# Softmax sums in attention: a tile moved to VectorE, a TensorE sum kept for odd units only, copies moved to ScalarE

## The chip, the cores and the metric

The kernel runs on one core of a Trainium2 chip. The metric is the time of one execution on the device in microseconds (us); with several runs, their median.

## The reference

Two rounds of the same pair of layers, in float32: attention over 2048 tokens with 32 heads of 32 columns, then a small feed-forward part for 8 chosen tokens. The change touches the attention alone.

```python
q, k, v = ...(layernorm(x) @ wqkv)            # 32 heads of 32, S = 2048, D = 1024
scores = einsum("bhqd,bhkd->bhqk", q, k) * 32 ** -0.5
p = softmax(scores, axis=-1)
x = x + einsum("bhqk,bhkd->bhqd", p, v) @ wo
x = x + (8 rows picked by a router: SwiGLU of those rows, the others get layernorm(x))
```

## The kernel before

**Units and steps.** The attention of a layer is 32 units of 16 steps. A unit `u` is a group of 4 heads and a chunk of 512 queries (`g, qc = divmod(u, 4)`); a step `s` takes one tile of 128 keys: `s = 16 * u + kt`. In step `s` TensorE makes the scores of 4 heads (`scores`, tile `pre`, L775), ScalarE turns them into `P[s]` by two exponentials of 128x1024 (L1256), and one step later TensorE multiplies `P[s]` with the values (`pv_step`, tile `pv`, L1154). In the same step TensorE also makes scores of the unit after the next (`pre_pair`, tile `st`, L736): two products, then two more, of which ScalarE takes one (`first`, L739) and VectorE three (L741, L743), for the row maxima that the exponentials of that later unit subtract. The banks of `st` are three, so a product waits until an earlier one was read; the second of the second pair waits for ScalarE's L739 of the same step.

**The sums.** Softmax also needs the sum of `P` over the keys, which are 16 tiles times 128 partitions. Tables of numbers say what is done at which step of a unit (16 and more is in the next unit). `SUMS` serves all but the last two units of a layer. A "merge" adds one tile to another by an accumulating DMA that GpSimd issues (L1192), an "add" adds a tile to the accumulator `ACC[u]` on GpSimd (128x2048, L1164). Each unit has 6 merges and 8 adds. Tile 14, with tile 15 merged in, isn't added: at step 22 (`SUM_AT`) TensorE sums it by products with ones (`sum_mm`, L1201), VectorE copies the result (`store_sum`, L1211, tile `sm`) and SyncE stores it (`sd`). Of units 0 to 28 the accumulator goes through VectorE in steps 24 to 31: four times a transposition in blocks of 32x32 (L1170, tile `turned`) and a reduction of it into `FOLD` (L1178). Once for every four units (`total`), and once after unit 28, TensorE sums `FOLD` over partitions with one product (L1186), which goes to `sd2`. At the end `sd + sd2` is inverted.

**Outputs.** One step after a unit's last tile the output `PV[u]` is copied from PSUM to tile `o` (`store_o`, L1206) and stored. This copy and that of the sum are VectorE's for units 2 to 29; for units 0, 1, 30 and 31 they are ScalarE's (`PLAIN <= u <= NU - 3`).

**Order and buffers.** The order on each engine is that in which the code issues: within a step `emit(s, "pre")`, the scores and exponentials, `pv_step`, `emit(s, "mid")`, `emit(s, "end")`. Each engine works through its queue in that order and waits at an instruction whose inputs or buffer aren't ready. `P` has 9 buffers (`PB`). A new tile gets the buffer that the program let go of first, and its exponential waits until the last reader or writer of the old tile is done, which for a tile that was merged is the landing of the DMA.

## Time and profile before

| what | us |
|---|---|
| median of 3 runs | 4354.69 |
| the runs | 4342.66, 4354.69, 4354.86 |
| the profiled execution, its own time | 4348.58 |
| its span from the first to the last instruction | 4346.8 |
| TensorE busy in the span | 4307.6 |
| VectorE, ScalarE, GpSimd busy in the span | 3045.8, 2880.2, 3270.6 |

The two attention stages lie at about 565 to 1917 us and 2719 to 4076 us of the span. TensorE's granted clock is 0.997 of full speed over the span. A busy time is the union of the instructions' records; the records of neighbours on one engine can overlap by some tens of nanoseconds, since an engine starts the next instruction before the record of the last ends. On VectorE, ScalarE and TensorE the distance from start to start is therefore the better price.

### The profile page before, as it was taken

Reading aid. Unit: us, or ns where it says so; the run is one execution under the profiler, and the core shown is the slowest. Engines: PE = TensorE matmul, PEld = TensorE weight load, DVE = VectorE, ACT = ScalarE, POOL = GpSimd, SP = SyncE. Lnnn points to the kernel's source line nnn. Section 1 sums busy time; section 2 is a strip of 40 time slices with the busy share of each in tenths; the row PEclk is TensorE's granted clock in tenths of the full one; section 3 lists DMA queues with packets and bytes.
Section 4 is the critical chain, followed back from the end, with each engine's and each line's share of the span. In section 5 each row is a group of like instructions: output and inputs, shape, how many; then the busy total and the mean of one; then the engine's idle time right before and its main releaser. Section 6 shows DMA issues by size and latency. Waiting matters only on the chain.

```text
span 4346.8 us, 75763 instructions
## 1 busy us (share of the span) xinstructions
PE 4307.6 (99%) x28255; PEld 2612.5 (60%) x28255; DVE 3045.8 (70%) x5607; ACT 2880.2 (66%) x3447; POOL 3270.6 (75%) x1367
## 2 busy tenths in 40 slices
PE   9999999999999999999999999999999999999998
PEld 7888755555555555558877787555555555555583
DVE  3322678888888898887422215888888888888863
ACT  3333289999999999960222222999999998999510
POOL 5544479999999999925634443899999999999152
PEclk9999999999999999999999999999999999999999
DMA  7877588998999989868698774999989999998698
GB/s 222 268 241 230 158 183 190 200 204 193 210 199 192 214 191 199 174 181 244 180 313 305 263 215 129 206 196 196 210 190 201 200 195 201 198 195 175 185 266 342
DMA packets 362638, 918.70 MB, mean 211 GB/s; under 512 B 48220, under 2 KB 184924, under 8 KB 305934
## 3 DMA queue, kind: packets, MB, share of 16 engines
q0 software_dynamic: 53312, 384.39, 44.2%
q1 hardware_dynamic: 291646, 490.07, 37.2%
q10 hardware_dynamic: 17312, 39.40, 3.3%
q8 instruction: 222, 3.64, 0.3%
q14 instruction: 146, 1.20, 0.1%
HBM read 395.35 MB, written 134.67 MB: 122 GB/s over the span
## 4 chain that ended last, share of the span: by engine, by line
PE 93%; DMA 3%; DVE 1%; issue 1%; POOL 1%; ACT 0%; SPq 0%; POOLq 0%; ACTq 0%; DVEq 0%
PE pv L1154 23%; PE pre L775 22%; PE st L932 17%; PE st L736 15%; PE pre L1438 6%; PE pre L932 5%; PE st L1201 1%; PE pv L567 1%; DMA wraw<-in_A_wqkv_dram 1%; PE pre L757 1%; PE pv L932 1%; DMA ord<-rd 0%; PE third L775 0%; DMA P<-P 0%; PE st L607 0%
## 5 line engine op out<-in xcount | busy, mean ns | idle before, releaser
L1164 POOL TENSOR_TENSOR acc<-acc,P 128x2048 f32<-128x2048 f32 x420 | 2058.7, 4902 | 9.4
L1256 ACT ACTIVATE P<-pre 128x1024 f32<-128x1024 f32 x2016 | 1955.1, 1024 | 24.8 <-PE pre L775 17.6
L743 DVE TENSOR_REDUCE nm<-st 128x1 f32<-128x512 f32 x1920 | 1321.0, 688 | 51.3 <-PE st L736 7.9
L775 PE MATMUL pre<-q,ks 64*128 64x512 f32 (+1 forms) x8064 | 1123.1, 395 | 2.4 <-ACT P L1256 2.4
L1154 PE MATMUL pv<-P,v 128*32 128x512 f32 x8192 | 1087.2, 605 | 0.0
L736 PE MATMUL st<-ks,q 64*128 64x512 f32 x2880 | 874.3, 432 | 2.0 <-issue 2.0
L775 PEld LDWEIGHTS pre<-q,ks 64*128 64x128 f32 (+1 forms) x8064 | 770.5, 186 | 159.9 <-ACT P L1256 32.1
L741 DVE CUSTOM_DVE_ANT_0 first<-st,first 128x512 f32<-128x512 f32 x960 | 664.0, 692 | 241.3 <-PE st L736 231.9
L739 ACT ACTIVATE first<-st 128x512 f32<-128x512 f32 x960 | 574.5, 598 | 184.4 <-PE st L736 99.6
L736 PEld LDWEIGHTS st<-dt,q 64*128 64x128 f32 x960 | 175.7, 183 | 798.2 <-DVE nm L741 727.4
L736 PEld LDWEIGHTS st<-ks,q 64*128 64x128 f32 x2880 | 487.9, 185 | 46.0 <-issue 2.3
L736 PE MATMUL st<-dt,q 64*128 64x512 f32 x960 | 476.3, 496 | 0.0
L1192 POOL DMA_DIRECT2D P<-P x366 | 373.9, 1022 | 111.3 <-PE st L736 39.6
L947 DVE TENSOR_TENSOR lo<-st,hi 128x512 fp32r<-128x512 f32 x128 | 88.4, 691 | 513.9 <-ACT hi L946 469.0
L832 POOL TENSOR_TENSOR ohl<-wraw,ord 128x2048 fp32r<-128x2048 f32 (+1 forms) x54 | 222.3, 4120 | 241.5 <-ACT ord L827 205.7
L946 ACT CAST hi<-st 128x512 fp32r<-128x512 f32 x128 | 75.2, 587 | 444.5 <-PE st L932 352.5
L832 POOL TENSOR_TENSOR wl<-wraw,wh 128x2048 fp32r<-128x2048 f32 (+1 forms) x54 | 222.5, 4123 | 170.6 <-ACT wh L831 165.2
L1154 PEld LDWEIGHTS pv<-P,v 128*32 128x32 f32 x8192 | 164.0, 108 | 263.7 <-issue 257.0
L1164 POOL TENSOR_TENSOR acc<-P 128x2048 f32<-128x2048 f32 x62 | 317.9, 5128 | 0.1
L181 POOL TENSOR_TENSOR rs<-mv,eps_c 128x1 f32<-128x1 f32 x64 | 27.7, 433 | 296.3 <-DVE mv L179 296.3
L1438 PE MATMUL pre<-woh,ohl 128*128 128x512 f32 x960 | 223.9, 390 | 3.0 <-DVE pre L1472 2.2
L1369 ACT CAST ohl<-ord 128x1024 fp32r<-128x1024 f32 x32 | 33.6, 1051 | 273.4 <-DVE ord L1360 114.3
(422 smaller groups left out, 5317.4 us busy)
## 6 DMA issues: line engine op xcount, KB each, us to landing
P<-P POOLq DMA_DIRECT2D x366, 1024.0 KB, 10.1
wraw<-in_A_wqkv_dram SPq DMA_DIRECT2D x96, 1024.0 KB
q<-qh SPq DMA_DIRECT2D x256, 128.0 KB
ks<-kh SPq DMA_DIRECT2D x112, 256.0 KB
fw<-in_B_w_down_dram SPq DMA_DIRECT2D x17, 1024.0 KB
vd<-vn SPq DMA_DIRECT2D x32, 512.0 KB
qh<-hi SPq DMA_DIRECT2D x64, 256.0 KB
ql<-lo SPq DMA_DIRECT2D x64, 256.0 KB
```

The costliest lines, as they stand in the source:

```text
L736: pe.matmul(p, Q[u][rows, i, 0, qt * 128:(qt + 1) * 128], keys, start=True, stop=True, tile_position=(64 * b, 0))
L739: act.activation(side, ps[jj], AF.Relu)
L741: dve.tensor_tensor_reduce(side, ps[jj], side, 1.0, -3.0e38, OP.add, OP.max, NM[u][:, 0, h, qt:qt + 1])
L743: dve.tensor_reduce(NM[u][:, 1 + k, h, qt:qt + 1], ps[1 - jj], axis=AX.X, op=OP.max)
L775: pe.matmul(p[:, b * 512:(b + 1) * 512], KS[(u // QC) % 2][rows, i, slot, kt * 128:(kt + 1) * 128], Q[u][rows, i, slot, :], start=(slot == ...
L832: pool.tensor_tensor(wl[:, sl], raw[:, sl], wh[:, sl].bitcast(F32), op=OP.subtract)
L932: pe.matmul(p, *pair(a, l, r), start=(a == 0 and k == 0), stop=(a == KD - 1 and k == 2))
L1154: pe.matmul(PV[u][32 * h:32 * h + 32, :], V[g, kt // 4][:, kt % 4, 32 * h:32 * h + 32], P[s][:, h, :], start=(kt == 0), stop=(kt == NT - 1 ...
L1164: (dve if on_dve else pool).tensor_tensor(o, a, P[u * NT + k].rearrange("p h c -> p (h c)"), op=OP.add)
L1192: pool.dma_start(P[u * NT + a], P[u * NT + b], accum_op=OP.add)
L1256: act.activation(P[s][:, 2 * i:2 * i + 2, :].rearrange("p h c -> p (h c)"), p, AF.Exp, scale=SCALE)
L1438: pe.matmul(p[:, bl], l[:, a, :], r[a][:, bl], start=(k == 0 and a == 0), stop=(k == 2 and a == KD - 1))
```

## The change

`SPLIT_SUMS` takes the place of `SUMS` for units 0 to 28. Tile 15 isn't merged any more: VectorE turns and reduces it straight from `P` in steps 16 to 23 (`turn` with `raw`, from `RAW_AT`), into a second `FOLD`, and `total` makes two products in one PSUM tile instead of one. The merges become 12<-11 and 14<-13 where they were 13<-12 and 14<-15. The last entry of the table, the add of tile 14, is for even units alone, which have no `sum_mm` and no stored sum any more (their places in `sd` are filled with zeros ahead of the attention). Odd units leave out that add and keep `sum_mm` of tile 14. `store_o` and `store_sum` copy on ScalarE in all units, both through tile `o`. The two lines at the end of the stage that load half of the sums move by two steps.

```diff
+SPLIT_SUMS = (
+    (3, "merge", 2, 1), (5, "merge", 4, 3), (6, "add", 0, 5), (7, "add", 6), (9, "merge", 7, 8), (9.5, "add", 2), (11, "merge", 9, 10),
+    (11.5, "add", 4), (13, "merge", 12, 11), (14, "add", 7), (15, "merge", 14, 13), (16, "add", 9), (18, "add", 12), (20, "add", 14))
+TURNED_TILE = 15
+RAW_AT = 16
...
+    sums = BEHIND_SUMS if left == 1 else SUMS if u >= TURNED else SPLIT_SUMS[:-1] if u % 2 else SPLIT_SUMS
...
+    if u >= TURNED or u % 2:
+        ev += [(SUM_AT, "mid", 5, "sum", ())]
+    if u < TURNED:
+        ev += [(at + k, "pre", 1, "turn", (k, raw)) for at, raw in ((RAW_AT, True), (TURN_AT, False)) for k in range(8)]
+        ev += [(TURN_AT + 7, "mid", 5, "total", ())]
...
-                    dve.transpose(TURN[u], ACC[u][:, 512 * h:512 * h + 512])
+                    dve.transpose(TURN[u], P[u * NT + TURNED_TILE][:, h, :] if raw else ACC[u][:, 512 * h:512 * h + 512])
...
-                pe.matmul(p, lanes, FOLD.pop(u // QC), start=True, stop=True, tile_position=(0, 0))
+                for raw in (True, False):
+                    pe.matmul(p, lanes, FOLD.pop((u // QC, raw)), start=raw, stop=not raw, tile_position=(0, 0))
...
-                (dve.tensor_copy if PLAIN <= u <= NU - 3 else act.copy)(o, PV.pop(u))
+                act.copy(o, PV.pop(u))
...
-                (dve.tensor_copy if PLAIN <= u <= NU - 3 else act.copy)(t, p)
+                act.copy(t, p)
...
-                store_sum(u, sum_mm(u), aw.tile([128, 512], F32, name="sm", bufs=1))
+                store_sum(u, sum_mm(u), aw.tile([128, 512], F32, name="o", bufs=1))
...
+            for i in range(2):
+                dma(half_of(sd, i).rearrange("(p two) c -> p (c two)", two=4), DT[i][32:64].bitcast(F32).rearrange("p a c -> p (a c)"))
...
-                if s == NS - 20:
-                    shared["first"] = aw.tile([128, 512], F32, name="sm", bufs=1)
+                if s == NS - 22:
+                    shared["first"] = aw.tile([128, 512], F32, name="o", bufs=1)
```

GpSimd, from the add of tile 4 of unit 12 (an even one) to the second merge of unit 13. Before, the tiles of unit 12 are P_10738 (4), P_10988 (11), P_11023 (12), P_11056 (13), P_10847 (7), P_11089 (14), P_11122 (15) and P_10921 (9):

```order
L1164 TENSOR_TENSOR acc_10836<-acc_10836,P_10738 128x2048
L1164 TENSOR_TENSOR acc_10836<-acc_10836,P_10988 128x2048
L1192 DMA P_11056<-P_11023 128x2048
L1164 TENSOR_TENSOR acc_10836<-acc_10836,P_10847 128x2048
L1192 DMA P_11089<-P_11122 128x2048
L1164 TENSOR_TENSOR acc_10836<-acc_10836,P_10921 128x2048
L1192 DMA P_11225<-P_11193 128x2048
L1164 TENSOR_TENSOR acc_10836<-acc_10836,P_11056 128x2048
L1192 DMA P_11289<-P_11256 128x2048
```

The same stretch of the changed kernel; here unit 12 has P_10813 (4), P_11067 (11), P_11102 (12), P_10926 (7), P_11134 (13), P_11168 (14) and P_11000 (9):

```order
L1174 TENSOR_TENSOR acc_10914<-acc_10914,P_10813 128x2048
L1204 DMA P_11102<-P_11067 128x2048
L1174 TENSOR_TENSOR acc_10914<-acc_10914,P_10926 128x2048
L1204 DMA P_11168<-P_11134 128x2048
L1174 TENSOR_TENSOR acc_10914<-acc_10914,P_11000 128x2048
L1174 TENSOR_TENSOR acc_10914<-acc_10914,P_11102 128x2048
L1204 DMA P_11310<-P_11276 128x2048
L1174 TENSOR_TENSOR acc_10914<-acc_10914,P_11168 128x2048
L1204 DMA P_11377<-P_11343 128x2048
```

The unit's last two merges have moved ahead by one add each; two adds, not one, now stand between the last of them and the next unit's first merge. In an odd unit the add of tile 14 is missing.

ScalarE, steps 6 to 8 of unit 14 (the unit after an odd one), with the semaphores waited for (DMASW is the landing of a merge, Pool is GpSimd). Before, P_11899, P_11944 and P_11985 are the steps 6, 7 and 8:

```order
L1256 ACTIVATE P_11899<-pre_11900 128x1024 [waits DMASW3_49,PE_49,Activation_49]
L1256 ACTIVATE P_11899<-pre_11906 128x1024 [waits PE_49]
L739 ACTIVATE first_11936<-st_11938 128x512 [waits PE_49]
L1256 ACTIVATE P_11944<-pre_11945 128x1024 [waits PE_49,Pool_49]
L1256 ACTIVATE P_11944<-pre_11951 128x1024 [waits PE_49]
L739 ACTIVATE first_11976<-st_11978 128x512 [waits DVE_49,PE_49]
L1256 ACTIVATE P_11985<-pre_11986 128x1024 [waits DMASW4_49,PE_49,Activation_49]
```

The same steps of the changed kernel, where they are P_11991, P_12037 and P_12078:

```order
L1270 ACTIVATE P_11991<-pre_11992 128x1024 [waits PE_49,Pool_49]
L1270 ACTIVATE P_11991<-pre_11998 128x1024 [waits PE_49]
L1223 COPY o_12019<-st_12014 128x512 [waits DMAHW1_49,PE_49,Activation_49]
L749 ACTIVATE first_12028<-st_12030 128x512 [waits PE_49]
L1270 ACTIVATE P_12037<-pre_12038 128x1024 [waits DMASW4_49,PE_49,Activation_49]
L1270 ACTIVATE P_12037<-pre_12044 128x1024 [waits PE_49]
L749 ACTIVATE first_12069<-st_12071 128x512 [waits DVE_49,PE_49]
L1270 ACTIVATE P_12078<-pre_12079 128x1024 [waits PE_49]
```

The copy of the sum stands between two steps. The landing of the unit's own first merge (2<-1, the semaphore DMASW4 in both) was waited for at step 8 and is now at step 7; after an even unit it is still at step 8.

VectorE, the first two steps after unit 13. Before (the copy of `o` stands at the end of step 0 of unit 14):

```order
L743 TENSOR_REDUCE nm<-st 128x1 x2
L741 ISA first,nm<-st,first 128x512
L741 ISA nm 128x1
L743 TENSOR_REDUCE nm<-st 128x1
L1206 COPY o<-pv 128x512
L743 TENSOR_REDUCE nm<-st 128x1
L741 ISA first,nm<-st,first 128x512
```

In the changed kernel:

```order
L753 TENSOR_REDUCE nm<-st 128x1 x2
L1181 STREAM_TRANSPOSE turned<-P 128x512
L751 ISA first,nm<-st,first 128x512
L751 ISA nm 128x1
L753 TENSOR_REDUCE nm<-st 128x1 x2
L1189 TENSOR_REDUCE fold_11274<-turned 128x4x4
L751 ISA first,nm<-st,first 128x512
```

Every step has one transposition or one reduction of it between its third maximum and the next step's first line 751, as before only the second half of a unit's steps had.

## Rows read from the trace of the kernel before

**Rows 1.** The page's busy times, and a table of windows of the steady part of the first attention stage (busy us of each engine, granted TensorE clock, share of the DMA engines, GB/s).

```profile
PE 4307.6 (99%) x28255; PEld 2612.5 (60%) x28255; DVE 3045.8 (70%) x5607; ACT 2880.2 (66%) x3447; POOL 3270.6 (75%) x1367
...
1100.00:1400.00 300.00, 300.00 (x2310) 154.29 (x2308) 265.34 (x538) 277.31 (x338) 294.76 (x99) 1.00 0.93 200
```

**Rows 2.** The chain of work that ended last, in order of time, around a `sum_mm` whose copy is VectorE's (start, us, what), and two of the steps after it.

```profile
1003.60 1.00 PE pv L1154 x8
1004.59 0.86 PE st L1201 x8
...
1007.06 1.00 PE pv L1154 x8
...
1009.66 0.99 PE pv L1154 x8
...
1012.26 1.00 PE pv L1154 x8
```

**Rows 3.** The same view at a `total`.

```profile
1113.20 1.00 PE pv L1154 x8
1114.19 0.41 PE st L1186 x2
1114.61 0.59 PE st L736 x2
...
1116.37 1.00 PE pv L1154 x8
```

**Rows 4.** The same view where ScalarE makes the copies: the output of unit 0 (first four rows), that of unit 1 (next three), the sum of unit 0 (last two).

```profile
602.38 0.99 PE pv L1154 x8
...
604.75 0.53 PE st L736 x2
605.28 0.99 PE pv L1154 x8
...
608.04 1.00 PE pv L1154 x8
...
645.46 0.99 PE pv L1154 x8
...
648.34 1.00 PE pv L1154 x8
...
650.94 1.00 PE pv L1154 x8
...
618.47 1.00 PE pv L1154 x8
...
621.95 1.06 PE pv L1154 x8
```

**Rows 5.** ScalarE's timeline at the copy of unit 0's output and at that of its sum (start, us, engine, line, instruction, and in brackets the idle time before it).

```profile
601.80 1.94 ACT L1256 ACTIVATE P<-pre 128x1024 f32<-128x1024 f32 x2
603.63 0.59 ACT L1206 COPY o<-pv 128x512 f32<-128x512 f32 x1
604.09 0.63 ACT L739 ACTIVATE first<-st 128x512 f32<-128x512 f32 x1
...
620.39 0.59 ACT L1211 COPY sm<-st 128x512 f32<-128x512 f32 x1 [0.60 <-PE st L1201]
```

**Rows 6.** A table of windows (columns as in Rows 1): steps in which VectorE turns the accumulator, then steps in which it doesn't; and VectorE's timeline over a step of the first kind.

```profile
1009.20:1030.00 20.80, 20.80 (x162) 10.62 (x161) 20.34 (x41) 19.49 (x25) 20.72 (x8) 1.00 0.62 125
1030.00:1046.00 16.00, 16.00 (x126) 8.32 (x122) 12.59 (x26) 15.23 (x20) 16.00 (x8) 1.00 1.00 220
...
1014.37 0.70 DVE L1170 STREAM_TRANSPOSE turned<-acc 128x512 f32<-128x512 f32 x1
1015.00 0.69 DVE L741 CUSTOM_DVE_ANT_0 first<-st,first 128x512 f32<-128x512 f32 x1
...
1015.62 1.44 DVE L743 TENSOR_REDUCE nm<-st 128x1 f32<-128x512 f32 x2
1016.98 0.68 DVE L1178 TENSOR_REDUCE fold<-turned 128x16 f32<-128x512 f32 x1
1017.61 0.69 DVE L741 CUSTOM_DVE_ANT_0 first<-st,first 128x512 f32<-128x512 f32 x1
```

**Rows 7.** GpSimd's timeline from a unit's add of tile 7 to the next unit's merge 2<-1.

```profile
1029.85 4.89 POOL L1164 TENSOR_TENSOR acc<-acc,P 128x2048 f32<-128x2048 f32 x1
1034.40 1.18 POOL L1192 DMA_DIRECT2D P<-P  x1
1035.02 5.17 POOL L1164 TENSOR_TENSOR acc<-acc,P 128x2048 f32<-128x2048 f32 x1
1039.94 1.08 POOL L1192 DMA_DIRECT2D P<-P  x1
```

**Rows 8.** Merges from issue to landing (the last number, us): the one issued at 1039.94, the one at 1013.65, then all of them; and who waited for a merge (us, times).

```profile
P<-P POOLq DMA_DIRECT2D x1, 1024.0 KB, 11.0
...
P<-P POOLq DMA_DIRECT2D x1, 1024.0 KB, 8.1
...
DMA to landing us min/median/max: 6.9/10.1/14.6
...
  ACT P L1256: 2.3, 4
```

**Rows 9.** ScalarE's timeline at step 7 of the unit whose merge 2<-1 is the one issued at 1039.94.

```profile
1049.05 1.94 ACT L1256 ACTIVATE P<-pre 128x1024 f32<-128x1024 f32 x2
```

More of the change, by code (lines that the diff above doesn't have):

```diff
@@ L56, with unit_events @@
     ((1, 18), (1, 21), (2, 18), (3, 3)), ((2, 14), (2, 17), (2, 20), (3, 3)))]
-def unit_events(left):
+def unit_events(u):
+    left = NU - 1 - u
     if left == 0:
@@ L63, in unit_events @@
     ev = []
-    for at, what, k, *other in (SUMS, BEHIND_SUMS)[left == 1]:
+    sums = BEHIND_SUMS if left == 1 else SUMS if u >= TURNED else SPLIT_SUMS[:-1] if u % 2 else SPLIT_SUMS
+    for at, what, k, *other in sums:
         args = (k, *other) if what == "merge" else (k, *(other or [None]), what == "vadd")
         ev.append((int(at), "end", at % 1, "merge" if what == "merge" else "add", args))
-    ev += [(SUM_AT, "mid", 5, "sum", ())]
-    if left == NU - TURNED:
-        ev += [(TURN_AT + k, "pre", 1, "turn", (k,)) for k in range(8)] + [(TURN_AT + 7, "mid", 5, "total", ())]
+    if u >= TURNED or u % 2:
[3 more added lines that the diff above has]
+        ev += [(TURN_AT + 7, "mid", 5, "total", ())]
     return ev
-EVENTS = [unit_events(i) for i in range(NU - TURNED + 1)]
+EVENTS = [unit_events(u) for u in range(NU)]
 @with_exitstack
@@ L1164, in acc_add, with turn @@
                 (dve if on_dve else pool).tensor_tensor(o, a, P[u * NT + k].rearrange("p h c -> p (h c)"), op=OP.add)
-            def turn(u, k):
+            def turn(u, k, raw):
                 h, back = divmod(k, 2)
+                key = (u // QC, raw)
                 if not back:
                     TURN[u] = aw.tile([128, 512], F32, name="turned", bufs=1)
-                    dve.transpose(TURN[u], ACC[u][:, 512 * h:512 * h + 512])
+                    dve.transpose(TURN[u], P[u * NT + TURNED_TILE][:, h, :] if raw else ACC[u][:, 512 * h:512 * h + 512])
                     return
                 if u % QC == 0 and h == 0:
-                    FOLD[u // QC] = aw.tile([128, 256], F32, name="fold", bufs=1)
+                    FOLD[key] = aw.tile([128, 256], F32, name=f"fold{int(raw)}", bufs=1)
                     if u // QC == NG - 1:
-                        dve.memset(FOLD[u // QC], 0.0)
+                        dve.memset(FOLD[key], 0.0)
                 i, j = divmod(u % QC, 2)
-                out = FOLD[u // QC].rearrange("p (i c j t h) -> p i j h t c", i=2, c=4, j=2, t=4)[:, i, j, h]
+                out = FOLD[key].rearrange("p (i c j t h) -> p i j h t c", i=2, c=4, j=2, t=4)[:, i, j, h]
                 dve.tensor_reduce(out, TURN.pop(u).rearrange("p (t c r) -> p t c r", t=4, c=4), axis=AX.X, op=OP.add)
-                if h == 3:
+                if h == 3 and not raw:
                     ACC.pop(u)
@@ L1185, in total @@
                 p = ps_st()[0:32, 0:256]
-                pe.matmul(p, lanes, FOLD.pop(u // QC), start=True, stop=True, tile_position=(0, 0))
-                t = aw.tile([128, 512], F32, name="sm", bufs=1)[0:32, 0:256]
+                for raw in (True, False):
+                    pe.matmul(p, lanes, FOLD.pop((u // QC, raw)), start=raw, stop=not raw, tile_position=(0, 0))
+                t = aw.tile([128, 256], F32, name="sm", bufs=1)[0:32]
                 dve.transpose(t, p)
@@ L1239, in emit @@
                     if 0 <= v < NU:
-                        todo += [(kt + NT * back, pri, fn, args, v) for (k, pos, pri, fn, args) in EVENTS[min(NU - 1 - v, NU - TURNED)]
+                        todo += [(kt + NT * back, pri, fn, args, v) for (k, pos, pri, fn, args) in EVENTS[v]
                                  if k == kt + NT * back and pos == where]
@@ L1247, in layer @@
             load_ones(1)
+            for i in range(2):
+                dma(half_of(sd, i).rearrange("(p two) c -> p (two c)", two=4), DT[i][32:64].bitcast(F32).rearrange("p a c -> p (a c)"))
             for i in range(2):
@@ L1270, in rest_of_step @@
                     shared["sum"] = sum_mm(NU - 1)
-                if s == NS - 20:
-                    shared["first"] = aw.tile([128, 512], F32, name="sm", bufs=1)
+                if s == NS - 22:
+                    shared["first"] = aw.tile([128, 512], F32, name="o", bufs=1)
                     sum_load(shared["first"], 0)
-                if s == NS - 17:
+                if s == NS - 19:
                     recip(shared["first"], 0)
```

## The prediction

> **What bounds the kernel now.** I read the page's busy times first, then the windows of the attention stages, then the chain of work that ended last. In the steady part of attention TensorE is busy for 300.00 us of 300 at a granted clock of 1.00 [rows 1], and the chain runs over nothing but TensorE, one product after the other. So a step costs what TensorE's products cost: 1012.26 - 1009.66 = 2.60 us from one `pv` to the next [rows 2]. I use 2.605, since neighbouring steps read 2.60 and 2.61. The others aren't far behind: in the same 300 us GpSimd is busy for 294.76, ScalarE for 277.31 and VectorE for 265.34 [rows 1]. The change takes work from TensorE and GpSimd and gives it to VectorE and ScalarE, which both release PSUM banks that TensorE writes next. The questions are what the removed products were worth, and which of the added instructions makes TensorE wait.
>
> **The sums that go.** A step with `sum_mm` takes from one `pv` to the next 1007.06 - 1003.60 = 3.46 us, and the products themselves stand in the chain with 0.86 [rows 2]. So each one left out gives 0.86 us, all of it on the path. In units 0, 2, ..., 28 that is 15 a layer, 30 in all. In unit 0 the copy was ScalarE's already, and there the step costs 0.08 more (below); gain 30 x 0.86 + 2 x 0.08 = 26.0 us.
>
> **Two products in `total`.** Now such a step takes 1116.37 - 1113.20 = 3.17, 0.56 over a plain one: 0.41 for the product and 0.16 in the next `st`, which takes 0.59 where others take 0.43 [rows 2, 3]. I read the 0.16 as a wait for a bank; a second product of the same size covers it. So I put the second at 0.41 - 0.16 = 0.25, and at most at another 0.56. There are 8 a layer: 16 x 0.25 = 4.0 us (up to 9.0).
>
> **Outputs copied by ScalarE.** Units 0 and 1 show it before the change, with the same neighbours on TensorE and ScalarE. The copy begins when the last `pv` and the exponentials are through (603.63), and the following L739 begins at 604.09 [rows 5]. The last `st` product of that step waits for this L739: the pair takes 0.53 where others take 0.24, and the step takes 605.28 - 602.38 = 2.90, the one at unit 1 648.34 - 645.46 = 2.88 [rows 4]. The step after is 2.76 in the first case and 2.60 in the second. I take 0.28 a copy, and 0.44 with the step after as the upper bound. VectorE's copies, which go, gave TensorE no wait and so give nothing back. 28 outputs a layer move (units 2 to 29): 56 x 0.28 = 15.7 us (up to 24.6). Below, the bound is zero, if in later units something else holds TensorE at that point anyway.
>
> **Sums copied by ScalarE.** Here ScalarE stands idle for 0.60 us until the sum is there [rows 5], so most of the copy lies in time that was lost anyway. From the end of one `pv` to the end of the next it is 621.95 + 1.06 - 618.47 - 1.00 = 3.54 us against 3.46 where VectorE copies [rows 2, 4]: 0.08 for each of the 28 odd units that change (3 to 29, both layers), 2.2 us. Both copies now share the one buffer `o`; between the two lie six steps, 15.6 us, for a store that SyncE issues at once.
>
> **Tile 15 on VectorE.** Eight instructions more for each of 58 units, 464 in all, less two copies of about the same length in each of units 2 to 29 (the sum copy of an even unit goes altogether). By starts, a turn and what follows it are 0.63 us apart (1014.37 to 1015.00, 1016.98 to 1017.61) [rows 6]: 5.0 us more in a unit of some 42.5. That all lies beside TensorE if a step with a turn still fits into 2.605. Steps with one show that it does: VectorE is busy there for 20.34 us of 20.80 and TensorE keeps its pace, while without turns it is 12.59 of 16.00 [rows 6], which is where the new ones go. I cost it at nothing. The cover is thin: what follows the turn (L741) holds a bank of the next step's first products, so a turn that ends late moves TensorE by as much.
>
> **GpSimd.** Odd units lose an add, 28 of 4.9 us [rows 7]; merges stay at six a unit. GpSimd isn't what bounds the step, so this gives nothing by itself. But the order of the merges changes, and with it who waits for which landing: that is the second rival.
>
> **Sum.** -26.0 + 4.0 + 15.7 + 2.2 = -4.1 us. The profiled execution took 4348.58 us (span 4346.8), so 4344.5. It lies between the runs shown and 6.1 below their median; on the median's scale the forecast is 4354.69 - 4.1 = 4350.6, that is -0.1%, which a measurement of this kernel can't tell from no change (some 0.3%, 13 us).
>
> **Rival 1: VectorE becomes the bound.** With a turn in every step its share goes from about nine tenths to 98% [rows 1, 6]. If each of the 464 new steps lost 0.05 us, that is 23.2 us: 4373.8. For: no step with a turn has had ScalarE's output copy in it yet, and an engine that never rests can't catch up after a stall. Against: eight such steps in a row already run without loss, and VectorE loses a copy in every unit. It decides from 0.04 us a step on (464 x 0.04 = 18.6, net slower than 0.3%).
> The Trainium skill (VectorE: DVE Perf Modes, The DRAIN you can't avoid) has a rule against this part: the next VectorE operation doesn't start until the pipeline of the last has emptied. By that the four long instructions of a step would take 0.69 + 1.44 + 0.69 = 2.82 us by their records, 0.2 over TensorE's step, and the change would cost an estimated 464 x 0.2 = 93 us, 4444. The starts in rows 6, 0.62 to 0.63 apart, speak against it, and so do the steps with turns; I give that no more than a small part of this rival's chance.
>
> **Rival 2: ScalarE waits for a merge.** After an odd unit the exponential of step 7 now waits for the landing of that unit's own merge 2<-1, one step earlier than before. In the trace such a merge is issued at 1039.94 and lands 11.0 us later, at 1050.94 [rows 7, 8]; the exponential of step 7 starts at 1049.05 [rows 9]. If that stays, ScalarE and behind it TensorE stop for up to 1.9 us in 28 even units (2 to 28, both layers): +53.2 us, 4403.8. Against: the merge took 11.0 us because the one before it, issued at 1034.40, was still under way. In the new order that one comes behind the add of tile 7 with one add less ahead of it, about 4.5 us earlier, and lands before 1039.94 or close to it. A merge issued with none ahead took 8.1, so it would land at 1048.0, 1 us in time; the least is 6.9 [rows 8]. What speaks for it is the spread of landings (up to 14.6) and the DMA engines' share of 0.93. It decides from landings of about 9.8 us on.
> The Trainium skill (DMA: Bandwidth & Descriptors, Anatomy of one DMA) would rule the wait out: about 2 us and the bytes at 436 GB/s, an estimated 4.4 us for such a tile, which would leave this rival no chance and the sum as it is. The trace doesn't agree: no merge took less than 6.9.
>
> **Rival 3: the output copy is hidden.** If in later units it costs TensorE nothing, the sum is -26.0 + 4.0 + 2.2 = -19.8: 4334.9. Against it stand three of four readings near 0.28.
>
> **Rival 4: even units don't become shorter.** The 0.86 us of `sum_mm` are also a pause in which ScalarE, VectorE and GpSimd catch up. GpSimd has 41.8 us of work (98.25%) in a unit of 16 x 2.605 + 0.86 = 42.5 us; an even unit keeps that work and would take 16 x 2.605 + 0.28 = 42.0. If the pause is needed, the 26 us aren't gained while the 21.9 are paid: 4376.6. Against: the odd unit behind it has one add less.
>
> **How the numbers follow.** Forecast 0.60, rival 1 0.12, rival 2 0.12, rival 3 0.10, rival 4 0.06. Predicted: 4350.6. Range: below to rival 3, 4334; above past rivals 1 and 4 to 4385, which leaves out rival 2 and the tail of rival 1. The forecast's own bounds (output copies up to 24.6, `total` up to 9.0) reach 4364.5. Faster by over 0.3% (under 4341.6): rival 3 and a little of the forecast, 0.13. Slower (over 4367.8): rivals 2 and 4 and most of rival 1, 0.27. Within: 0.60.
>
> **What would show it.** In the chain, even units without L1201 and steps of 2.6 us at their place; at each `total` two products and about 3.4 us; a step of 2.9 us after every unit. VectorE's windows near 98% busy with TensorE at 300.00 of 300. On ScalarE no exponential at step 7 that waits for a merge: if "ACT P <- DMA P<-P" in the waits is more than some us, rival 2 is right. Steps of 2.65 us or more all through, with TensorE released by L751, would be rival 1. The forecast is wrong at its root if steps between these places change their length.

## The result and the profile after

The changed kernel takes 4390.8 us (median of 6 runs, 4384.99 to 4394.46); the kernel before, run beside it, takes 4353.86. The ratio on record is 1.0098 with an interval of 1.0083 to 1.0112, that is about 43 us slower, where 4 us less were forecast. (The two medians themselves are 36.9 us apart, the two profiled executions 42.7.) The profiled execution has a span of 4389.1 us, 42.3 more than before, and all of it lies in the two attention stages.

The costs that the prediction named are there, about as large as it said. This is the chain of work that ended last, after (start, us, what): first the start of an odd unit behind an even one, then the step with `sum_mm` behind an odd unit, then a `total`.

```profile
1041.27 1.00 PE pv L1164 x8
1044.15 1.00 PE pv L1164 x8
...
1057.18 1.00 PE pv L1164 x8
1059.79 1.00 PE pv L1164 x8
1062.39 1.00 PE pv L1164 x8
...
1273.98 0.99 PE pv L1164 x8
1274.97 0.86 PE st L1213 x8
1275.83 0.43 PE st L746 x2
...
1277.59 0.99 PE pv L1164 x8
...
1123.57 0.99 PE pv L1164 x8
1124.57 0.84 PE st L1198 x4
1125.41 0.43 PE st L746 x2
...
1127.02 0.99 PE pv L1164 x8
```

The step of the output copy takes 1044.15 - 1041.27 = 2.88. Behind an even unit the steps in which the sum stood are 2.61 and 2.60 long. The step with the sum takes 3.61 (3.46 before, [rows 2]), `total` 3.45 (3.17, [rows 3]). Over both layers the medians are 2.89, 3.60 and 3.45, and of steps without any of this 2.605, as before. So by measured sizes the four terms are -26.0 + 16 x 0.28 + 56 x 0.285 + 28 x 0.13 = -1.9 us. Some 44 us are left, and they are not in these terms. Added up over both layers, the distances from one `pv` to the next are too long by 16 us at step 1, 3 at step 5 and 23 at step 7 of the third unit of each group of four, by 7 at step 8 of the second and by 3 at step 7 of the first; the kernel before lost some 6 us at steps of its own. The page, the windows and the waits of the changed kernel show what stands behind them (a group: busy us, mean ns | idle us before it and its releasers; a wait: us in total, times, longest):

```profile
PE 4321.3 (98%) x28047; PEld 2598.3 (59%) x28047; DVE 3250.1 (74%) x5961; ACT 2910.2 (66%) x3529; POOL 3141.6 (72%) x1339
...
PE 86%; DMA 7%; issue 3%; POOL 1%; ACT 1%; DVE 1%; SPq 0%; POOLq 0%; ACTq 0%; DVEq 0%
...
L1270 ACT ACTIVATE P<-pre 128x1024 f32<-128x1024 f32 x2016 | 1957.7, 1027 | 74.4 <-DMA P<-P 40.2
L1174 POOL TENSOR_TENSOR acc<-acc,P 128x2048 f32<-128x2048 f32 x392 | 1913.0, 4880 | 79.3 <-DMA P<-P 71.5
```

```profile
1100.00:1400.00 300.00, 295.18 (x2226) 148.87 (x2220) 281.08 (x562) 273.11 (x339) 270.70 (x92) 1.00 0.92 194
...
1301.30:1343.50 42.20, 42.18 (x324) 21.48 (x321) 40.87 (x83) 39.78 (x50) 40.27 (x14) 1.00 0.95 198
```

```profile
POOL acc L1174 <- DMA P<-P: 71.5, 55, 3.6
ACT P L1270 <- DMA P<-P: 40.2, 41, 2.4
```

ScalarE's exponentials waited for merges for 2.3 us before [rows 8] and wait for 40.2 now. GpSimd's adds, which hardly waited at all, wait for 71.5. In the first window (columns as in [rows 1]) TensorE is no longer busy throughout, and VectorE has 19 us of 300 left at an unchanged clock. The second is a unit without a stall: VectorE is busy for 97% of it, and TensorE for all of it. So VectorE with a turn in every step doesn't hold TensorE.

One stall, read through. GpSimd's timeline from the last merges of unit 17 to the first of unit 18 (the second and the third unit of a group of four):

```profile
1332.95 1.19 POOL L1204 DMA_DIRECT2D P<-P  x1
1333.57 5.18 POOL L1174 TENSOR_TENSOR acc<-acc,P 128x2048 f32<-128x2048 f32 x1
1338.13 1.46 POOL L1204 DMA_DIRECT2D P<-P  x1
1338.84 5.37 POOL L1174 TENSOR_TENSOR acc<-acc,P 128x2048 f32<-128x2048 f32 x1
1343.40 1.65 POOL L1204 DMA_DIRECT2D P<-P  x1
1348.69 4.57 POOL L1174 TENSOR_TENSOR acc<-acc,P 128x2048 f32<-128x2048 f32 x1 [3.64 <-DMA P<-P]
1353.72 4.61 POOL L1174 TENSOR_TENSOR acc<-acc,P 128x2048 f32<-128x2048 f32 x1 [0.47 <-DMA P<-P]
1358.25 0.87 POOL L1204 DMA_DIRECT2D P<-P  x1
```

The three merges from issue to landing (the last number, us), and SyncE's timeline over unit 17 (`ks` are keys, 256 KB a load; `dt` their differences, 64 KB):

```profile
P<-P POOLq DMA_DIRECT2D x1, 1024.0 KB, 15.6
P<-P POOLq DMA_DIRECT2D x1, 1024.0 KB, 15.5
P<-P POOLq DMA_DIRECT2D x1, 1024.0 KB, 16.0
...
1309.31 0.32 SPq L115 DMA_DIRECT2D ks<-kh  x1
1322.00 3.62 SPq L115 DMA_DIRECT2D nmx<-nmr  x4
1328.24 1.14 SPq L115 DMA_DIRECT2D q<-nmx  x2
1329.42 1.11 SPq L115 DMA_DIRECT2D ks<-kl  x1
1330.58 2.47 SPq L115 DMA_DIRECT2D ks<-kh  x2
1333.09 0.85 SPq L115 DMA_DIRECT2D ks<-kl  x1
1333.98 0.43 SPq L115 DMA_DIRECT2D ks<-kh  x1
1334.45 1.05 SPq L115 DMA_DIRECT2D dt<-kd  x2
```

In the code a unit's key loads stand one a step, from step 6 to step 13. In the trace SyncE's queue stands still behind the transfers of the row maxima (`nmx`), and then five of the six large loads and both small ones go out within some 6 us, at steps 10 to 12, beside the merges 9<-10 and 12<-11. The first units of a group show the same burst, and so does the kernel before, where only the merge 9<-10 falls beside it.

ScalarE's timeline at steps 1 and 7 of unit 18:

```profile
1348.65 1.94 ACT L1270 ACTIVATE P<-pre 128x1024 f32<-128x1024 f32 x2 [2.20 <-DMA P<-P]
...
1366.97 1.94 ACT L1270 ACTIVATE P<-pre 128x1024 f32<-128x1024 f32 x2 [1.43 <-DMA P<-P]
```

The merge 9<-10, issued at 1332.95, lands 15.6 us later at 1348.5. For this landing GpSimd's add of tile 9 waits 3.64 us and ScalarE's step 1 waits 2.20. The merge 12<-11 lands at 1353.6, and the add of tile 12 waits 0.47. Behind these adds stands the next unit's merge 2<-1: issued at 1358.25, 14.7 us after the unit's first exponential (10.0 is usual before), it lands 8.6 us later at 1366.86, and ScalarE's step 7 waits 1.43 for it. Where the kernel before passed this point, GpSimd went from one instruction to the next without a gap [rows 7].

### The profile page after: what moved, and what is told of

Read it like the earlier page. It is cut to its first block, busy times and chain, and to the rows that moved or that the text cites. A ratio compares the mean times of both kernels' runs of the same rounds, so it can differ in the third digit from the quotient of the medians.

```text
span 4389.1 us, 75570 instructions
## 1 busy us (share of the span) xinstructions
PE 4321.3 (98%) x28047; PEld 2598.3 (59%) x28047; DVE 3250.1 (74%) x5961; ACT 2910.2 (66%) x3529; POOL 3141.6 (72%) x1339
## 4 chain that ended last, share of the span: by engine, by line
PE 86%; DMA 7%; issue 3%; POOL 1%; ACT 1%; DVE 1%; SPq 0%; POOLq 0%; ACTq 0%; DVEq 0%
PE pv L1164 21%; PE pre L785 19%; PE st L942 16%; PE st L746 13%; PE pre L1452 7%; PE pre L942 5%; DMA P<-P 5%; DMA wraw<-in_A_wqkv_dram 1%; ACT P L1270 1%; PE st L1213 1%; PE pre L767 1%; PE pv L577 1%; POOL ohl L842 1%; PE pv L942 1%; POOL acc L1174 0%
## 5 line engine op out<-in xcount | busy, mean ns | idle before, releaser
L1270 ACT ACTIVATE P<-pre 128x1024 f32<-128x1024 f32 x2016 | 1957.7, 1027 | 74.4 <-DMA P<-P 40.2
L1174 POOL TENSOR_TENSOR acc<-acc,P 128x2048 f32<-128x2048 f32 x392 | 1913.0, 4880 | 79.3 <-DMA P<-P 71.5
L746 PE MATMUL st<-ks,q 64*128 64x512 f32 x2880 | 888.2, 434 | 0.0
L785 PEld LDWEIGHTS pre<-q,ks 64*128 64x128 f32 (+1 forms) x8064 | 755.5, 186 | 219.4 <-ACT P L1270 91.3
L751 DVE CUSTOM_DVE_ANT_0 first<-st,first 128x512 f32<-128x512 f32 x960 | 663.7, 691 | 69.0 <-PE st L746 66.3
L749 ACT ACTIVATE first<-st 128x512 f32<-128x512 f32 x960 | 577.7, 602 | 131.3 <-PE st L746 67.6
L1204 POOL DMA_DIRECT2D P<-P x366 | 388.1, 1060 | 215.8 <-PE st L746 136.0
L1189 DVE TENSOR_REDUCE fold<-turned 128x16 f32<-128x512 f32 x464 | 314.8, 679 | 0.1
```

Of the source, the lines that this page charges most:

```text
L746: pe.matmul(p, Q[u][rows, i, 0, qt * 128:(qt + 1) * 128], keys, start=True, stop=True, tile_position=(64 * b, 0))
L749: act.activation(side, ps[jj], AF.Relu)
L751: dve.tensor_tensor_reduce(side, ps[jj], side, 1.0, -3.0e38, OP.add, OP.max, NM[u][:, 0, h, qt:qt + 1])
L785: pe.matmul(p[:, b * 512:(b + 1) * 512], KS[(u // QC) % 2][rows, i, slot, kt * 128:(kt + 1) * 128], Q[u][rows, i, slot, :], start=(slot == ...
L1174: (dve if on_dve else pool).tensor_tensor(o, a, P[u * NT + k].rearrange("p h c -> p (h c)"), op=OP.add)
L1204: pool.dma_start(P[u * NT + a], P[u * NT + b], accum_op=OP.add)
```

## The experiments

Two theories were put first. **M**: the merges land late and ScalarE waits for their buffers. **V**: VectorE is full. From the second set on, **G** stood beside M: GpSimd falls behind by itself, for want of a pause in even units. Times below are ratios to the kernel before on the same chip, with their interval; "us" is the ratio less 1, of 4350. The last two columns are the waits of ScalarE's exponentials and of GpSimd's adds for merges, in the profiled execution.

| run | ratio | us | ScalarE waits | GpSimd waits |
|---|---|---|---|---|
| changed kernel | 1.0098 (1.0083 to 1.0112) | +43 | 40.2 | 71.5 |
| e1_copies_back | 1.0103 (1.0084 to 1.0123) | +45 | 43.1 | 67.6 |
| e2_copies_alone | 1.0034 (1.0023 to 1.0046) | +15 | none shown | none shown |
| e3_copy_behind | 1.0080 (1.0062 to 1.0098) | +35 | 29.3 | 69.6 |
| e4_no_key_loads | 1.0017 (1.0007 to 1.0027) | +7 | 9.5 | 11.4 |
| e5_keys_early | 1.0232 (1.0213 to 1.0251) | +101 | 78.6 | none shown |
| e6_five_merges | 1.0150 (1.0129 to 1.0172) | +65 | 53.5 | 25.6 |
| e7_before_no_keys | 0.9989 (0.9979 to 0.9998) | -5 | 1.5 | none shown |
| e8_sum_in_all | 1.0077 (1.0060 to 1.0094) | +33 | 15.5 | 44.1 |
| e9_keys_spread | 1.0138 (1.0121 to 1.0155) | +60 | 48.3 | 6.8 |
| e10_merge_first | 1.0193 (1.0176 to 1.0210) | +84 | 73.0 | 7.3 |
| e11_spread_behind | 1.0082 (1.0066 to 1.0099) | +36 | 37.3 | 10.1 |
| e12_keys_late_behind | 1.0068 (1.0054 to 1.0083) | +30 | 28.5 | 40.9 |
| e13_keys_late | 1.0056 (1.0041 to 1.0072) | +24 | 22.9 | 39.1 |
| e14_keys_late_behind_sums | 1.0070 (1.0056 to 1.0084) | +30 | 26.3 | 43.2 |
| e15_keys_later | 1.0009 (1.0000 to 1.0018) | +4 | 12.8 | 22.1 |
| e16_keys_placed | 1.0114 (1.0099 to 1.0129) | +50 | 43.0 | 43.7 |
| e17_keys_off_first | 1.0105 (1.0090 to 1.0120) | +46 | 49.3 | 44.6 |

A second table shows the mechanism (first layer, medians over units 4 to 27, worked out from GpSimd's and ScalarE's timelines): how long the merges 9<-10, 12<-11 and 14<-13 of a group's second unit take to land (before: 9<-10, 13<-12, 14<-15), and when the merge 2<-1 of the third unit is issued after that unit's first exponential, and how long it takes.

| run | landings, us | merge 2<-1 issued at | lands after |
|---|---|---|---|
| before | 13.8, 8.7, 10.5 | 10.0 | 10.4 |
| changed kernel | 14.4, 14.6, 14.9 | 14.0 | 8.7 |
| e4_no_key_loads | 8.0, 7.9, 8.5 | 10.4 | 7.3 |
| e6_five_merges | 14.8, 14.9 | 14.6 | 7.1 |
| e9_keys_spread | 12.2, 11.8, 12.1 | 11.1 | 8.7 |
| e10_merge_first | 9.8, 9.8, 11.5 | 10.3 | 10.1 |
| e16_keys_placed | 14.0, 14.0, not shown | 13.0 | 9.4 |

### The copies

**e1_copies_back** gives the copies of outputs and sums back to VectorE in the changed kernel, **e2_copies_alone** moves them to ScalarE in the kernel before, **e3_copy_behind** puts the output copy of the changed kernel behind the next step's L749.

```diff
-                act.copy(o, PV.pop(u))
+                (dve.tensor_copy if PLAIN <= u <= NU - 3 else act.copy)(o, PV.pop(u))
```

```diff
+                if held:                      # e3: one step later, behind pre_pair(*pr, 0, side)
+                    store_o(held.pop(), aw.tile([128, 512], F32, name="o", bufs=1))
```

> The changed kernel with the copies of outputs and sums back on VectorE (for units 2 to 29), the rest as changed. Theory M (ScalarE waits for P buffers until merges land, some 44 us; ScalarE's copies cost 0.28 and 0.13 us a piece): 56 x 0.28 + 28 x 0.13 = 19 us come back if VectorE still has room for the copies beside a turn in every step, so about 4372 against 4391; the waits for landings stay. Rival V (VectorE is full and that is where the time went): two copies of 0.6 us more a unit lengthen it, up to 56 x 0.6 + 28 x 0.6 = 50 us slower than the changed kernel, about 4441, and the waits name VectorE.

> The kernel before with only the copies moved to ScalarE. Theory M with the copies at 0.28 and 0.13 us: 56 x (0.28 + 0.13) = 23 us slower than before, about 4377, a step of 2.9 us after every unit. Rival C (the copies cost more in later units than in units 0 and 1, and are behind most of the 44 us not forecast): 50 us or more slower, 4405. If a copy is hidden in later units: 4354.

> The changed kernel with the copy of the output issued behind the next step's L749 instead of ahead of it, so that L749 isn't late. Theory M: the 0.28 us a unit shrink to 0.1 or less, 56 x 0.2 = 11 us faster than the changed kernel, about 4380; the waits for landings stay. Rival: the copy costs the same wherever it stands in ScalarE's queue, 4391; or the next pv waits for its bank and it costs more.

e2 costs 15 us (10 to 20 by the interval; 23 were expected), with steps of 2.89 behind each unit and 3.55 at each sum: about the price that the prediction gave the copies, in a kernel without a stall. e1 gains nothing, and neither of its two forecasts came. The waits for merges stay, and where VectorE turns in every step its copy costs as much as ScalarE's. VectorE's timeline in e1 at an output copy:

```profile
1130.13 0.69 DVE L751 CUSTOM_DVE_ANT_0 first<-st,first 128x512 f32<-128x512 f32 x1
...
1131.35 0.68 DVE L1218 COPY o<-pv 128x512 f32<-128x512 f32 x1
1131.95 0.68 DVE L753 TENSOR_REDUCE nm<-st 128x1 f32<-128x512 f32 x1
1132.55 0.68 DVE L1189 TENSOR_REDUCE fold<-turned 128x16 f32<-128x512 f32 x1
1133.14 0.68 DVE L751 CUSTOM_DVE_ANT_0 first<-st,first 128x512 f32<-128x512 f32 x1
```

From one L751 to the next it is 3.01 us there instead of 2.60, and the step of TensorE behind it is about 2.95 long. So one step with a copy and a turn is too much for VectorE, while a turn in every step is not: theory V holds for that step alone. e3 comes out 8 us lower, where 11 were expected, but the intervals overlap. The copy itself got cheaper by less: the two steps at a unit's end take 2.66 and 2.76 where they took 2.89 and 2.60, which is 0.07 less, some 4 us for 56 units.

### Loads, and GpSimd's pause

**e4_no_key_loads** leaves out the loads of the keys of groups 2 to 7 in the changed kernel (the attention of these groups then works with keys of earlier ones); **e7_before_no_keys** does so in the kernel before.

```diff
-                if g + 1 < NG:
+                if g + 1 < 2:
                     if qc < 2:
                         loads.extend((load_k, g + 1, h, i) for h in (2 * qc, 2 * qc + 1) for i in range(3))
```

> The changed kernel without the loads of keys (and of their differences) for the head groups 2 to 7 of each layer: the keys of groups 0 and 1 are used again, so the attention of the later groups isn't the reference's. Those loads run in units 0 and 1 of each four. Theory M with the loads as a part of the cause (stalls are seen in units 1 and 2 of each four): merges land in time, most of the 44 us come back, 4345 to 4360. If the closer merges alone are the cause, the stalls stay where they are: 4385 to 4391. Rival V: no change, 4391.

> Control: the kernel before without the key loads of groups 2 to 7 (the attention of those groups then works with the keys of earlier ones, so its result is another). Theory M: before, the loads meet only merges four steps apart at the end of a unit and cost next to nothing, so 4338 to 4346, at most 8 us less than the kernel before; the loss of 35 us to the loads belongs to the new order of merges. Rival (the loads cost time in both kernels alike): some 30 us less than before, about 4315.

Without these loads the changed kernel loses 7 us instead of 43, its merges land after 8 us even where they stand two steps apart, and the waits nearly go:

```profile
POOL acc L1174 <- DMA P<-P: 11.4, 9, 2.4
ACT P L1270 <- DMA P<-P: 9.5, 7, 2.3
```

What is left of the waits is beside loads too: the loads of group 1, in the first two units of each layer, stay in e4, and all nine waits of GpSimd's adds and 7.1 of ScalarE's 9.5 us lie in the second and third unit of a layer. The kernel before gains only 5 us by the same. So neither the new order of the merges nor the loads are enough: it takes both. e4 also speaks against G by itself: with the same adds in even units, but without loads, the merge 2<-1 goes out 10.3 to 10.5 us after its unit's first exponential in every kind of unit. And it rules out that VectorE's new instructions lengthen the landings, since e4 has them all.

**e8_sum_in_all** uses the short table in all units (TensorE sums tile 14 everywhere, GpSimd has an add less); **e6_five_merges** fills GpSimd's pause in odd units with the add of tile 13 in place of the merge 14<-13; **e10_merge_first** turns GpSimd's order.

```diff
-    sums = BEHIND_SUMS if left == 1 else SUMS if u >= TURNED else SPLIT_SUMS[:-1] if u % 2 else SPLIT_SUMS
+    sums = BEHIND_SUMS if left == 1 else SUMS if u >= TURNED else SPLIT_SUMS[:-1]             # e8
+    sums = BEHIND_SUMS if left == 1 else SUMS if u >= TURNED else ODD_SUMS if u % 2 else SPLIT_SUMS   # e6
...
-    (11.5, "add", 4), (13, "merge", 12, 11), (14, "add", 7), (15, "merge", 14, 13), (16, "add", 9), (18, "add", 12), (20, "add", 14))
+    (11.5, "add", 4), (13, "merge", 12, 11), (14, "add", 7), (15, "add", 13), (16, "add", 9), (18, "add", 12))                # e6, ODD_SUMS
+    (11.5, "add", 4), (13, "merge", 12, 11), (14, "add", 7), (15, "merge", 14, 13), (16, "add", 9), (19.5, "add", 12), (21.5, "add", 14))   # e10
```

> The changed kernel with the short table in all units: TensorE sums tile 14 in even units too (two copies of sums on ScalarE instead of one in two units), and GpSimd has one add less in every unit. It gives back the 26 us gain of the sums and about 2 us for their copies. Theory M: the merges stand where they stood, so the landings in units 0 and 1 of each group stay at 13 to 16 us and the stalls stay, less what GpSimd makes good by being early: 4395 to 4420. Rival G: GpSimd has 5 us of pause in every unit, the stalls of some 44 us go, and the time is 4370 to 4378.

> The changed kernel with five merges instead of six in odd units: tile 13 isn't merged into 14, GpSimd adds it in the time that the add left out in odd units leaves. Theory M: a seventh of a unit's bytes less in every second unit, so the stalls after odd units (steps 1 and 7 of the unit behind) go and those inside unit 1 of a group get smaller; half to three quarters of the 44 us, 4358 to 4370. Rival G: odd units lose the pause that GpSimd had there, all units then hold 98% work for it, and the time rises, above 4395.

> The changed kernel with GpSimd's order turned at one place: the next unit's merge 2<-1 stands ahead of the add of tile 12 and its merge 4<-3 ahead of the add of tile 14 (the adds move from steps 18 and 20 to 19.5 and 21.5). Bytes, landings and loads stay. Theory M+G: the merge 2<-1 no longer waits behind an add that waits for a landing, it is issued at its usual time in all units, and the stalls at step 7 and 8 go: 4350 to 4370, less what the tiles 12 and 14, which are held some 5 us longer, cost at other steps. Rival (ScalarE waits because the landings themselves are long): 4385 or more.

e8, at 4382.6 between the two forecasts, speaks for G as much as for M. It pays back the 26 us of the sums and 4 for their copies and by its ratio is still 9 us faster than the changed kernel (the intervals overlap; but it has 30 us more work on TensorE and isn't slower). In the second unit its merge 9<-10 takes 14.1 us (14.4 in the changed kernel), its 12<-11, which stands later there, 12.2 (14.6), and GpSimd's adds still wait 44.1 us, but ScalarE only 15.5: most of the wait doesn't reach the next unit, since GpSimd has time to make it good (the merge 2<-1 of the third unit goes out at 11.4 instead of 14.0). e6 is the counterpart, and there M was wrong: fewer bytes, but no pause, and 22 us more. Even the merge 2<-1 of a group's first unit goes out at 14.3. e10 puts that merge back to 10.3 in all units and is 41 us worse, as its rival said: ScalarE now waits at step 5 of the first and third unit and at step 7 of the second, for other merges. The likely reason, not taken apart, is that the tiles 12 and 14 are held longer and the adds behind them come later. This turn of the order doesn't remove the lateness.

### The place of the loads

All of these move the same bytes. The steps are those of the code; what SyncE's queue makes of them is told behind the runs. **e5_keys_early** issues the large loads at steps 0 to 5 of the first two units; **e9_keys_spread** all of them at every second step; **e11_spread_behind** adds the copy of e3.

```diff
+                if keys and s % 2:            # e9; e5: one a step from step 0
+                    f, *args = keys.pop(0)
+                    f(*args)
                 if loads:
```

> The changed kernel with the key loads of the next group in other steps: the twelve of 256 KB in steps 0 to 5 of the first two units of a group (before: steps 6 to 11), the four of 64 KB in steps 0 to 3 of the third (before: steps 12 and 13 of the first two). Same bytes, same merges. Theory M (the merges of steps 9 to 15 lie two steps apart, and with the key loads beside them the DMA engines are full, so they land after 13 to 16 us and hold P buffers): in units 0 and 1 of each group the merges of steps 11 to 15 land after about 9 us, most of the stalls go, and the time is 4345 to 4365, as without the loads (1.0017), unless the loads now hold up the merges of steps 3 and 5 instead. Rival G (GpSimd has no pause left in even units and falls behind by itself, so merges and adds start late): unchanged, about 4385 to 4392.

> The changed kernel with the key loads of a group at every second step of its first two units (1, 3, ... 15) instead of at each of steps 6 to 13; same bytes. Theory M+G (late landings of the merges 9<-10, 12<-11 and 14<-13 make GpSimd's adds of 9, 12 and 14 wait; the next unit's merge 2<-1, queued behind them, is issued up to 4 us late and ScalarE waits for its buffer; an even unit leaves GpSimd no time to catch up): the merges of steps 9 to 15 land after 10 to 12 us instead of 13 to 15, the merge 2<-1 is issued within 1 us of its usual time, and half or more of the 44 us goes, 4355 to 4372. Rival (the loads cost what they cost wherever they stand, since the DMA engines are full in these units): 4385 to 4395; or, if the merge 2<-1 itself now lands after more than 10 us, more than that.

> The spread key loads together with the output copy behind the next step's first relu on ScalarE, which by itself gave some 10 us. Both theories: some 10 us under the run with the spread loads alone; under M+G 4345 to 4362, so about the kernel before or a little under it.

In e5 the merges of steps 9 to 15 land after 7 to 8 us, as M wants, and GpSimd's adds wait for none; but now the merge 2<-1, issued on time at 10.4, lands after 13.4 us in a group's first unit and 13.0 in its second, and ScalarE waits up to 5.6 us at step 7 or 8:

```profile
ACT P L1271 <- DMA P<-P: 78.6, 26, 5.6
...
1118.00:1122.70 4.70, 1.47 (x11) 0.32 (x10) 2.79 (x7) 0.10 (x1) 4.62 (x2) 1.00 1.03 244
1122.70:1129.50 6.80, 5.82 (x26) 2.71 (x28) 1.90 (x4) 4.78 (x6) 1.60 (x3) 0.50 0.63 148
```

In e9 the same is left almost in the first unit alone (12.6 us). Both miss their forecast, and say why: this merge has only some 8 to 10 us to land. But not all of their time is waiting. The two windows of e5 (columns as in [rows 1]) lie around the end of one such stall: TensorE is busy for 1.47 us of 4.70, and then works for 6.8 us at a granted clock of 0.50, the lower of its two levels (1.2 of 2.4 GHz). Over the span the granted clock is 0.989 in e5 and 0.991 in e9, against 0.998 in the changed kernel. On 4450 and 4406 us that is an estimated 40 and 31 us, so the longer, rarer stalls of these two runs cost clock as well, and their us can't be read as waits alone. e11 comes out 24 us under e9, where 10 were expected, with waits of 37.3 instead of 48.3 and a clock of 0.994; it too misses its 4345 to 4362.

**e12** to **e15** then keep the loads away from it in the first unit: e12 and e13 issue them at two of three steps from step 7 on (e13 changes nothing else, e12 has the copy of e3, e14 also the sum copies back on VectorE); e15, otherwise as e14, starts at step 9 with every second step and takes three of four in the second unit.

```diff
+                if keys and (u % QC or kt > 6) and (kt % 3 != 2):                            # e12, e13, e14
+                if keys and (u % QC or kt > 7) and (kt % 4 != 3 if u % QC else kt % 2):      # e15
```

> The changed kernel with the output copy behind the next step's first relu on ScalarE, and the sixteen key loads of a group at two of three steps from step 7 of its first unit to step 13 of the second. Theory M+G: the stalls of the run with the spread loads lay in the first unit of each group, where a load beside the merge 2<-1 made it land after 12 us; with none there in steps 0 to 6 they go, and the merges of steps 9 to 15 land after 10 to 13 us: 4345 to 4360, some 30 us under the run with spread loads and the same copy. Rival (the loads cost what they cost, wherever they stand): 4380 or more.

> The same key loads without the move of the output copy: the changed kernel with nothing but the times of the loads changed. Theory M+G: 4353 to 4372, at least 20 us under the changed kernel, about as without the loads. Rival: 4385 to 4395.

> As the first of these, with the copies of the sums back on VectorE: 28 odd units by 0.13 us, so 3 to 4 us under it, 4342 to 4357 under theory M+G; level with the kernel before or up to 0.2% under it. Rival: 4377 or more.

> As the last, with the loads still later: every second step from step 9 of the first unit, then three of four steps of the second up to step 14. Theory M+G: within 8 us of the last, better if the merges of the first unit's steps 9 to 15 decide, worse if the second unit's merge 2<-1 (which has one step more) now lands after more than 10.5 us.

e13, with nothing but the place of the loads changed, gains 18 us of 43 over the changed kernel: less than expected, since the second unit's merge 2<-1 now lands after 11.7 us. The copy behind gains nothing there (e12), nor do the sum copies (e14); both miss their forecasts. e15, 26 us under e14 by the place of the loads alone, brings the waits to a third of the changed kernel's and the time, with the copies as in e14, level with the kernel before:

```profile
POOL acc L1179 <- DMA P<-P: 22.1, 30, 1.5
...
ACT P L1275 <- DMA P<-P: 12.8, 12, 2.4
```

**e16_keys_placed** and **e17_keys_off_first** were to take the rest, with the loads at chosen steps (otherwise as e15; the small ones move to the third unit).

```diff
+                if keys and kt in ((9, 11, 13, 15), (0, 2, 4, 7, 8, 10, 12, 14), (0, 1, 2, 3), ())[u % QC]:       # e16
+                if keys and kt in ((9, 11, 13, 15), (0, 1, 2, 8, 9, 11, 13, 15), (0, 1, 2, 3), ())[u % QC]:       # e17
```

> As the last run, with the loads placed by step: the twelve of 256 KB at steps 9, 11, 13, 15 of a group's first unit and 0, 2, 4, 7, 8, 10, 12, 14 of the second, the four of 64 KB at steps 0 to 3 of the third. Theory (a stall comes where a load stands beside a merge 2<-1, or so many beside the last three merges that GpSimd's adds wait): the merge 2<-1 of the second unit lands after 9.5 to 10.5 us instead of 10.4 to 12.6, that of the third is issued at its usual time, and of the 17 us of waits on ScalarE that were left at most 8 stay: 4337 to 4347, 0 to 0.2% under the kernel before. If the 64 KB loads, which have small packets, hold up the third unit's merge 2<-1, new waits at its step 7 take that back, and the time stays near 4351.

> As the run before, with the second unit's loads at steps 0, 1, 2, 8, 9, 11, 13, 15, none from 3 to 7, in which its merge 2<-1 is under way. By the theory that merge then lands after 8.5 to 9.5 us, and the last merges of the first unit, still under way at step 0, later than there by 1 us or so: within 5 us of it, lower if step 8 of the second unit still waited there.

e16 misses by some 50 us. e17 stays within 5 us of it, as expected, but the landing that it was to shorten, that of the second unit's merge 2<-1, takes 11.0 us and not 8.5 to 9.5. In both, SyncE lets five large loads and a small one go beside the second unit's last merges, where it is four and two in e15. These merges land after 14 us instead of 12.5, the third unit's merge 2<-1 goes out at 13.0 instead of 11.8, and it lands 1.3 us later, beside the small loads. Which of the two weighs more wasn't taken apart. No arrangement tried beats the kernel before.

In the traces of these runs, e5 apart, the loads that the code puts at steps 6 to 13 bunch up behind `nmx` and go out together at steps 9 to 12. The more large loads the second unit's bunch has, the later its merges 9<-10 and 12<-11 land (medians of the first layer): none, 8.0 and 7.9 us (e4); three, 11.5 to 12.2 (e9, e13); four, 12.5 and 12.7 (e15); five, 14.0 to 14.6 (e16, e17, the changed kernel). In e10 the bunch has five too, but both merges are issued 5 us or more after its last large load, and land after 9.8.

## Why the prediction was wrong, step by step

- **The sums that go, the second product, the output copies, VectorE's turns**: right. 2.605 for the steps of even units, 0.28 for 0.25, 0.285 for 0.28, and the undisturbed steps with a turn keep 2.605. So the 4444 us of rival 1's second paragraph didn't come: VectorE's instructions of 0.68 us start 0.60 apart in the rows of e1. The sum copies cost 0.13 for 0.08; in e2, where VectorE has no turn in that step, it is 0.08.
- **The step that failed** is the "against" of rival 2: "In the new order that one comes behind the add of tile 7 with one add less ahead of it, about 4.5 us earlier, and lands before 1039.94 or close to it", and so the merge 2<-1 would land after 8.1 us, 1 us in time. It holds only where no key loads are: behind a group's fourth unit, whose last merge lands after 9.7 us, the merge 2<-1 lands after 8.8 and step 7 hardly waits (1.0 us in all). The step took each landing for one that depends on the merges ahead of it in the queue, and took GpSimd's times of issue as given. In fact a merge beside key loads and two others takes 14 to 16 us, GpSimd's adds wait for it, and the merge 2<-1 behind them goes out up to 4.7 us late.
- **Rival 2** was the right place with part of the mechanism. ScalarE does wait at step 7 behind odd units (15.4 us), though only behind those with key loads, half of the 28; it waits as long at step 1 there for the merge 9<-10 (15.6 us), and less at step 5 (1.4) and at step 8 behind even units (4.6). The sign that the prediction set for rival 2, more than some us of "ACT P <- DMA P<-P", reads 40.2.
- **GpSimd** was costed at nothing because it doesn't bound the step. Rows 7 show it without a gap, and rival 4 named the pause, but priced it only at the 26 us that would not be gained. e8 and e6 show what the pause is for: with it GpSimd makes late landings good.
- **Rival 1** is out: VectorE is as full as it said, 97% in the unit shown, and TensorE isn't held.

The Trainium skill (DMA: Bandwidth & Descriptors, Queues, rings and completion order) says that each DMA engine takes turns, packet by packet, between the queues that have work for it. e4 and e5 fit it, though no run shows the turns themselves: the same merges, on their own queue, land after 8 us without SyncE's loads and 13 to 16 with them. The Trainium skill (DMA: Bandwidth & Descriptors, Anatomy of one DMA) would give 4.4 us (an estimate from 2 us and 436 GB/s for 1 MB); the least in any trace here is 6.9.

**Still open**: how a landing depends on the loads beside it beyond these medians, since the times of the loads differ between the runs too; what taking the loads out of the bunch would do, since no run changes SyncE's order against `nmx`; and whether a fitting place exists that also takes the last 13 us of ScalarE's waits in e15.

## What to carry to other kernels

When transfers are moved, redo their durations from what will run beside them at the new place: other queues' loads and each other, not from the durations at the old place. Read the times of the loads from the queue's timeline, not from the code: here loads written one a step went out five at a time. An engine that issues transfers and also waits for them needs a pause: in e8, which has one in every unit, late landings mostly stayed where they were, and in e6, which has none, they became late issues. A step that fits with one extra instruction says nothing on a step with two. And look at the granted clock before a run's time is put down to waits.

## What the runs showed that was not expected

The same 1 MB merge takes between 6.9 and 16.0 us in one trace. Three of them two steps apart land after 8 us each without key loads, and after 14 to 15 with a bunch of five loads of 256 KB and two of 64 beside them. The cost is steep: 78.6 us of ScalarE's waits in e5, 12.8 in e15, with every byte the same, and in e5 an estimated 40 us of lower clock on top.
